# A decode kernel's last sums: result columns taken from every fourth weight column, turned by VectorE in blocks of 32 in place of TensorE

## The chip, the cores and the metric

The kernel runs on one core of a Trainium2 chip. The metric is the device time in microseconds (us) of one execution. Lower is better. A profile of one execution (busy times, waits, transfers) stands beside the timed runs.

## What is computed

One token passes through attention over a cache and through a small MLP, and a gate mixes the two results. Cut to what matters, with x of 512 values, 32 heads of 128, 4096 cached keys and F = 1376:

```python
g = sigmoid((x * gate_w).sum(-1))
q = (x @ wq) as 32 heads of 128
p = softmax(q . k_cache * 128 ** -0.5)        # per head, over 4096 keys
a = (p . v_cache) as 4096 values @ wo         # wo: 4096 x 512
h = relu(x @ w1 + b1) ** 2                    # w1: 512 x 1376
b = h @ w2 + b2                               # w2: 1376 x 512
out = g * a + (1 - g) * b                     # 512 values, bf16
```

## The kernel before

**Stages.** Nearly all the work is reading the two caches and the weights, 78 MB in bf16. The 32 heads go in eight groups of four ("q" 0 to 7). For each group the keys K and the values V come as one transfer each of 4096 KB into two buffers for K and two for V; the list ORDER gives the sequence K0 K1 V0 K2 K3 V1 and so on up to V7. All of these, the loads of w1, wo and w2, and the write of the result are issued by SyncE (SP) in the order of its program. A load of K or V waits until the buffer's former content has been used, and what stands behind it in SP's program waits with it. wo comes in four quarters of 1024 KB: three go into one slot, each waiting for the products of the quarter before (s_wd), the last into a slot of its own. V7 comes in three pieces. After it SP issues the last quarter of wo and the five pieces of w2 (W2_PARTS: two of 512 KB, the remainder of 96 KB, two of 128 KB) with no wait between them, and then waits for s_f4, the sign that the result is ready to be written.

**TensorE** turns part of the keys (L460), forms their scores (L467), sums the values (pv, L501) and, for each pair of groups, turns the finished heads (turn, L519), spreads them over 128 partitions (spread, L525) and multiplies them with a quarter of wo (out_rows, L534). VectorE forms the scores of the other keys (L685 and L689) and ScalarE evicts the turned keys (L355) and takes the exponentials (L372).

**The last products.** The 512 results live as four columns of 128 partitions in the PSUM tile acc (pQ, columns 256 to 260): column j holds results 128 j to 128 j + 127. Each product is a pair: TensorE loads a block of 128 x 128 weights as the stationary operand and sends one column of activations through it, so the block's 128 columns become 128 partitions of one column of acc. out_rows(a) makes 32 such pairs for a quarter of wo. mlp_out(c) makes four for each row group of w2 in piece c. Both add into acc. At the end out_rows(1) and mlp_out(0) to mlp_out(4) follow each other on TensorE, each mlp_out waiting for its piece of w2.

Behind the last pair, VectorE adds the scaled second bias b2g to acc and writes accs, [128, 4] in bf16 (L756). TensorE turns accs into acc4, four rows of 128 in PSUM (L646), VectorE copies these into fin4 (L758), and SP writes fin4 to the output (L282): row j goes to results 128 j and up.

**The bias.** At the start ScalarE issues the small loads. b2r receives B_b2 as four rows of 128 (L329); it lies in the space of w1_sb, so SP's load of w1 (L271) waits for s_b2. TensorE turns b2r into four columns B2 of PSUM (L608) behind the first query products and ahead of the first keys; VectorE scales B2 by 1 - g into b2g (L673).

**Loads of weights with their columns apart.** Two places take a stationary operand whose columns are not neighbours in memory: the four matmuls that turn x into columns, xrow[:, t:DM:4] on one partition (L594), and the first MLP product, w1_sb[:, t, n:FG * 128:FG] with FG = 10 (L513), with its bias b1r[:, n:FG * 128:FG] (L509).

Of the kernel before, what the change touches and what calls it, by code (L numbers as in the profile page):

```python
# [5 lines left out]
def bass_gated_mix__gqa_block_cached__dense_activation_squared_relu__decode_kernel(  # L6
# [16 lines left out]
    bf16 = mybir.dt.bfloat16  # L23
# [6 lines left out]
    DM = 512  # L30
# [49 lines left out]
    with ctx:  # L80
        def sb(name, shape, dt):
            return ctx.enter_context(nc.sbuf_tensor(name, shape, dt))

        def pb(name, shape, dt):
            return ctx.enter_context(nc.psum_tensor(name, shape, dt))

        def sem(name):
            return ctx.enter_context(nc.semaphore(name))
# [5 lines left out]
        wo_sb = W[:, 0:2 * TB * DM].rearrange("p (g t n) -> p g t n", g=2, t=TB)  # L94
# [4 lines left out]
        w1_sb = sb("w1_sb", [128, 4, F], bf16)  # L99
# [7 lines left out]
        xrow = w1_sb[0:1, 0, 0:DM]  # L107
        grow = w1_sb[0:1, 1, 0:DM]
        b1r = sb("b1r", [1, F], bf16)
        b2r = w1_sb[0:4, 2, 0:128]  # L110
        oT = sb("oT", [GH, 128], bf16)
        o2 = sb("o2", [128, TB], bf16)
        fin4 = sb("fin4", [4, 128], bf16)
        zeros = sb("zeros", [128, 128], bf16)
        xb = sb("xb", [128, 4, 128], bf16)
        ident = sb("ident", [128, 128], bf16)
# [19 lines left out]
        hs = sb("hs", [128, FG + 1], bf16)  # L136
        b2g = sb("b2g", [128, 4], fp32)
        accs = sb("accs", [128, 4], bf16)
# [4 lines left out]
        pO = pb("pO", [128, 512], fp32)  # L143
# [6 lines left out]
        OT = KP[2][0:GH, 0:128]  # L150
        O2 = KP[3][:, 0:2 * TB].bitcast(fp32)
        Z = pO[:, 76:77]
        B2 = pO[:, 78:80].bitcast(bf16)
        acc4 = pO[0:4, 128:192].bitcast(bf16)
        QR = [pQ[:, :]] + [p[:, :].bitcast(fp32) for p in KP[0:3]] + [pQ[:, :]] * (NQ - QF)
        H = KP[0][:, 0:2 * (FG + 1)].bitcast(fp32)
        acc = pQ[:, 256:260]
# [3 lines left out]
        s_b = sem("s_b")  # L161
# [21 lines left out]
        s_b2 = sem("s_b2")  # L183
# [27 lines left out]
        s_oc = sem("s_oc")  # L211
        s_acc = sem("s_acc")
        s_as = sem("s_as")
        s_fin = sem("s_fin")
        s_f4 = sem("s_f4")
        s_out = sem("s_out")

# [11 lines left out]
        @block.sync  # L229
        def _(eng):  # L230
            def load_kv(n):
                kind, q = ORDER[n]
                if q >= 2:
                    done(kind, q - 2)
                if kind == "K":
                    eng.dma_start(KV[:, K_SLOT[q], :], k_q[q, :, :]).then_inc(s_k[q], 16)
                else:
                    at = 0
                    for m, sv in zip(V_PARTS[q], s_v[q]):
                        a, b = at * PB * 128, (at + m) * PB * 128  # L240
                        eng.dma_start(KV[:, V_SLOT[q], a:b], v_q[q, :, a:b]).then_inc(sv, 16)  # L241
                        at += m

            def done(kind, q):
                if kind == "K":
                    eng.wait_ge(s_sd, NP * (q + 1))
                    eng.wait_ge(s_t, GQ * (q + 1))
                else:
                    eng.wait_ge(s_pv, q + 1)

            def load_wo(g):
                if g == 0:
                    eng.wait_ge(s_qps, NQ)
                elif g < NG - 1:
                    eng.wait_ge(s_wd, g)
                a = 0 if g < NG - 1 else 1
                eng.dma_start(wo_sb[:, a, :, :], wo_v[g, :, :, :]).then_inc(s_wo[a], 16)  # L257

            def load_w2(n):
                a, b = W2_PARTS[n]  # L260
                if a < FG:
                    eng.dma_start(w2a[:, a:b, :], w2_v[:, a:b, :]).then_inc(s_w2[n], 16)  # L262
                else:
                    eng.dma_start(w2b[:, :], B_w2[FG * 128:F, :]).then_inc(s_w2[n], 16)  # L264

            for n in range(len(ORDER)):
                load_kv(n)
                if n == 2:
                    eng.wait_ge(s_z, 1)
                    eng.wait_ge(s_b2, 1)  # L270
                    eng.dma_start(w1_sb[:, :, :], w1_v[:, :, :]).then_inc(s_w1, 16)  # L271
                if n in WO_AT:
                    load_wo(WO_AT[n])
            load_wo(NG - 1)
            eng.wait_ge(s_sd, NP * NQ)
            load_w2(0)
            load_w2(1)
            load_w2(2)
            load_w2(3)
            load_w2(4)  # L280
            eng.wait_ge(s_f4, 1)
            eng.dma_start(out[0, 0, :].rearrange("(j p) -> j p", p=128), fin4[:, :]).then_inc(s_out, 16)  # L282


        @block.gpsimd
# [35 lines left out]
        def _(eng):  # L321
# [4 lines left out]
            eng.dma_start(xrow, A_x[0, :, :]).then_inc(s_x, 16)  # L326
            eng.dma_start(grow, gate_w.rearrange("(a n) -> a n", a=1)).then_inc(s_gw, 16)
            eng.dma_start(b1r[:, :], B_b1.rearrange("(a n) -> a n", a=1)).then_inc(s_b, 16)
            eng.dma_start(b2r, B_b2.rearrange("(j p) -> j p", p=128)).then_inc(s_b, 16)  # L329
            eng.wait_ge(s_xc, 1)  # L330
            eng.activation(xcolf[:, :], XC, ACT.Copy).then_inc(s_xf, 1)  # L331
            eng.wait_ge(s_xf, 1)
# [75 lines left out]
        def _(eng):  # L408
# [45 lines left out]
            def take(sm, n=1):  # L454
                eng.wait_ge(sm, n).then_inc(sm, -n)  # L455
# [73 lines left out]
            def out_rows(a):  # L529
                take(s_oc)  # L530
                take(s_wo[a], 16)
                for t in range(TB):
                    for j in range(4):
                        mm = eng.matmul(acc[:, j:j + 1], wo_sb[:, a, t, j * 128:(j + 1) * 128], o2[:, t:t + 1],  # L534
                                        start=False, stop=False, skip_group_check=True)
                mm.then_inc(s_wd, 1)

            def mlp_out(c, last=False):
                eng.wait_ge(s_w2[c], 16)
                a, b = W2_PARTS[c]  # L540
                for n in range(a, b):
                    M = 128 if n < FG else FR
                    w = w2a[:, n, :] if n < FG else w2b[:, :]
                    for j in range(4):
                        mm = eng.matmul(acc[:, j:j + 1], w[:, j * 128:(j + 1) * 128], hs[0:M, n:n + 1],  # L545
                                        start=False, stop=last, skip_group_check=True)
                if last:
                    mm.then_inc(s_acc, 1)
# [33 lines left out]

            at("rows")
            out_rows(0)
            branch("IS_GE", LAST, "next", "rows2")
            at("rows2")
# [6 lines left out]
            for t in range(4):  # L593
                mm = eng.matmul(XC[:, t:t + 1], xrow[:, t:DM:4], ident[0:1, 0:1], start=True, stop=True)  # L594
# [10 lines left out]
            eng.wait_ge(s_qc, QF)  # L605
            eng.wait_ge(s_b, 32)
            eng.wait_ge(s_ez, 1)
            eng.transpose(B2, b2r, ident[0:4, 0:4]).then_inc(s_b2, 1)  # L608

            part("k0")  # L610
            keys(0, extra[0])
# [24 lines left out]
            turn()  # L636
            spread()
            out_rows(1)
            eng.wait_ge(s_hs, 2)
            mlp_out(0)  # L640
            mlp_out(1)
            mlp_out(2)
            mlp_out(3)
            mlp_out(4, last=True)
            eng.wait_ge(s_as, 1)
            eng.transpose(acc4, accs[:, :], ident[:, :]).then_inc(s_fin, 1)  # L646


        @block.vector
        def _(eng):  # L650
# [20 lines left out]
            def bias():  # L671
                eng.wait_ge(s_b2, 1)
                eng.tensor_scalar(b2g[:, :], B2, omg[:, 0:1], None, ALU.mult).then_inc(s_bg, 1)  # L673

# [79 lines left out]
            eng.wait_ge(s_acc, 1)  # L754
            eng.wait_ge(s_bg, 1)
            eng.tensor_tensor(accs[:, :], acc[:, 0:4], b2g[:, :], ALU.add).then_inc(s_as, 1)  # L756
            eng.wait_ge(s_fin, 1)
            eng.tensor_copy(fin4[:, :], acc4).then_inc(s_f4, 1)  # L758

        body.close()  # L760
        nc.sync.wait_ge(s_out, 16)
# [28 lines left out]
```

## Time and profile before

| what | value |
|---|---|
| time, median of 3 runs | 190.74 us (190.69 to 190.84) |
| the profiled execution: its time | 190.55 us |
| its span, first to last instruction | 189.2 us |
| TensorE matmuls, busy | 137.1 us (72%) |
| TensorE weight loads, busy | 119.8 us (63%) |
| VectorE, busy | 123.0 us (65%) |
| ScalarE, busy | 116.0 us (61%) |
| read from HBM | 78.32 MB, 414 GB/s over the span |
| packets of SP's and ScalarE's loads (queue q1), share of 16 DMA engines | 97.1% |
| mean granted TensorE clock | 0.735 |
| in the last stage (184 to 187.5 us) | 0.50 |

Busy time counts an engine's instructions; PE is TensorE's matmuls and PEld its weight loads, which overlap. DVE is VectorE, ACT ScalarE, SPq SyncE's issuing of transfers. "out<-in" names the written and the read tile, "128*128" the size of the stationary operand, and in brackets stands how long the engine had been idle before and what ended that. The granted clock is a share of TensorE's full clock.

### The profile page before, as it was taken

The page shows a single profiled execution, that of the slowest core. Times are in us where ns is not written, and L with a number is a line of the kernel's source. Part 1 is how long each engine was busy: PE and PEld are TensorE (multiplying, and loading weights), DVE is VectorE, ACT ScalarE, POOL GpSimd, SP SyncE. Part 2 cuts the span into 40 slices and gives each one's busy share as a digit, 9 for nine tenths or more (in the row PEclk, how much of TensorE's full clock was granted, in tenths as well). Part 3 has the DMA queues.
Part 4 walks back from the last instruction along what each step waited for, and adds up shares of the span by engine and source line. Part 5 has one row for each costly group of instructions (what it writes and reads, how often), then busy time and mean ns, then how long its engine had stood idle before and what let it go on. Part 6 is the DMA issues. An engine that isn't in the chain of part 4 may idle for free. (4 is left out here: it accounts for less than half of the span.)

```text
span 189.2 us, 6234 instructions
## 1 busy us (share of the span) xinstructions
PE 137.1 (72%) x2688; PEld 119.8 (63%) x2688; DVE 123.0 (65%) x123; ACT 116.0 (61%) x243; POOL 6.0 (3%) x13
## 2 busy tenths in 40 slices
PE   0009297668849979969968797829868496889865
PEld 0003165537739779758958696829767495879864
DVE  0110099979969999996998299919990499701010
ACT  3004559948989986984987099708973298560000
POOL 4000000000700000000000000000000000000000
PEclk9999969958975975995795559655985579555555
DMA  6999999989989999999999999999999999999992
GB/s 225 437 444 443 443 443 426 443 361 483 440 360 436 443 443 440 417 436 430 443 424 409 423 443 443 436 436 436 414 445 409 416 443 443 438 388 416 421 388 78
DMA packets 4177, 78.47 MB, mean 415 GB/s; under 512 B 483, under 2 KB 837, under 8 KB 1094
## 3 DMA queue, kind: packets, MB, share of 16 engines
q1 hardware_dynamic: 4152, 78.32, 97.1%
q8 instruction: 7, 0.11, 0.2%
q14 instruction: 4, 0.03, 0.0%
q10 hardware_dynamic: 14, 0.01, 0.0%
HBM read 78.32 MB, written 0.00 MB: 414 GB/s over the span
## 5 line engine op out<-in xcount | busy, mean ns | idle before, releaser
L355 ACT ACTIVATE kT<-KP 128x1024 bf16<-128x1024 bf16 x80 | 75.3, 1041 | 26.1 <-PE KP L460 25.9
L685 DVE TENSOR_TENSOR w2a<-KV,qb 128x1536 f32<-128x1536 bf16 x32 | 56.3, 1760 | 19.4 <-DMA KV<-in_A_k_cache_dram 19.0
L460 PE MATMUL KP<-ident,KV 128*128 128x128 bf16 x640 | 59.6, 256 | 10.5 <-PEq L455 10.5
L460 PEld LDWEIGHTS KP<-ident,KV 128*128 128x128 bf16 x640 | 48.4, 116 | 14.1 <-issue 13.1
L689 DVE TENSOR_REDUCE S<-w2a 128x12 f32<-128x1536 f32 x32 | 56.1, 1753 | 1.1
L467 PE MATMUL pS<-qc,kT 128*128 128x4 bf16 x640 | 28.1, 166 | 13.0 <-PEq L455 11.0
L467 PEld LDWEIGHTS pS<-qc,kT 128*128 128x128 bf16 x640 | 24.6, 99 | 18.9 <-issue 17.6
L501 PEld LDWEIGHTS pO<-E,KV 128*128 128x128 bf16 x1024 | 29.3, 105 | 0.0
L501 PE MATMUL pO<-E,KV 128*128 128x4 bf16 x1024 | 28.4, 166 | 0.0
L372 ACT ACTIVATE E<-S,nM 32x128 bf16<-32x128 f32 x32 | 18.5, 578 | 0.9
L445 PE MATMUL pQ<-W,xb 128*128 128x512 bf16 x20 | 7.8, 532 | 7.2 <-DMA W<-in_A_wq_dram 6.1
L338 ACT ACTIVATE qb<-pQ 32x128 bf16<-32x128 f32 x20 | 5.4, 268 | 9.7 <-PE pQ L445 9.3
L361 ACT ACTIVATE S<-pS 32x80 f32<-32x80 f32 x32 | 7.3, 228 | 4.8 <-PE pS L467 4.2
L445 PEld LDWEIGHTS pQ<-W,xb 128*128 128x128 bf16 x20 | 2.2, 126 | 9.6 <-DMA W<-in_A_wq_dram 6.2
L372 ACT ACTIVATION_READ_ACCUMULATOR E<-S,nM 32x1 f32 x32 | 8.1, 252 | 0.0
L664 DVE TENSOR_SCALAR e<-ez 128x1 f32<-128x1 f32 x1 | 0.2, 153 | 10.8 <-ACT ez L387 10.8
L708 DVE RECIPROCAL rden<-pO 128x4 f32<-128x4 f32 x8 | 1.4, 174 | 8.2 <-PE pO L501 8.2
L594 PE MATMUL pO<-ident,w_sb 1*128 1x1 bf16 x4 | 0.3, 165 | 7.8 <-DMA w_sb<-in_A_x_dram 7.8
L497 PE MATMUL pO<-RS,onesf 128*128 128x4 f32 x16 | 4.3, 339 | 1.8 <-PEq L455 1.8
L655 DVE TENSOR_SCALAR xb<-zeros,xcolf 128x128 bf16<-128x128 bf16 x4 | 0.7, 248 | 7.5 <-ACT xcolf L331 7.5
L488 PE MATMUL pM<-identf,mp 128*1 128x128 f32 x8 | 3.0, 372 | 3.4 <-PEq L455 3.1
L497 PEld LDWEIGHTS pO<-RS,onesf 128*128 128x128 f32 x16 | 3.8, 298 | 2.1 <-issue 2.0
(75 smaller groups left out, 72.2 us busy)
## 6 DMA issues: line engine op xcount, KB each, us to landing
KV<-in_A_k_cache_dram SPq DMA_DIRECT2D x8, 4096.0 KB, 22.0
KV<-in_A_v_cache_dram SPq DMA_DIRECT2D x7, 4096.0 KB, 29.5
W<-in_A_wq_dram SPq DMA_DIRECT2D x1, 4096.0 KB, 13.4
W<-in_A_wo_dram SPq DMA_DIRECT2D x4, 1024.0 KB, 16.5
KV<-in_A_v_cache_dram SPq DMA_DIRECT2D x1, 2048.0 KB, 11.0
KV<-in_A_v_cache_dram SPq DMA_DIRECT2D x2, 1024.0 KB, 14.1
w_sb<-in_B_w_dram SPq DMA_DIRECT2D x1, 1376.0 KB, 24.4
w2a<-in_B_w_dram SPq DMA_DIRECT2D x2, 512.0 KB, 18.5
```

Of the source, the lines that this page charges most:

```text
L338: eng.activation(qb[rows(r), c, :], QR[c][rows(r), r * 128:(r + 1) * 128], ACT.Copy)\
L355: eng.activation(kT[:, n % NT, :], KP[n % NKP][:, :], ACT.Copy).then_inc(s_ev, 1)
L361: eng.activation(S[rows(r), q % NS, 0:YQ], S2[rows(r), :, r], ACT.Copy).then_inc(s_cp, 1)
L372: eng.activation(E[rows(r), q % 2, :, r], S[rows(r), q % NS, :], ACT.Exp, bias=nM[rows(r), q:q + 1], scale=SCALE, accum_out=RS[rows(r), q ...
L445: mm = eng.matmul(QR[c], xb[:, t, :], wq_sb[:, t, c * 512:(c + 1) * 512], start=(t == 0), stop=(t == 3))
L460: mm = eng.transpose(KP[(GQ * a + g) % NKP][:, y * 128:(y + 1) * 128], key(a, b), ident[:, :])
L467: mm = eng.matmul(pS[:, R * c:R * c + R], kT[:, (GQ * a + g) % NT, y * 128:(y + 1) * 128], qc2[:, a, :], start=True, stop=True)
L488: eng.transpose(MT, mp[:, a:a + 1], identf[:, :]).then_inc(s_mt, 1)
L497: eng.matmul(DEN[a], onesf[:, :], RS[:, a, :], start=True, stop=True)
L501: mm = eng.matmul(O[a], KV[:, V_SLOT[a], b * 128:(b + 1) * 128], E[:, a, COLUMN[b], :], start=(b == 0), stop=(b == NB - 1))
L685: eng.tensor_tensor(prod, KV[:, K_SLOT[q], x:x + XB * 128].rearrange("p (b d) -> p b d", d=128), qb[:, q, :].unsqueeze(1).to_broadcast([12 ...
L689: eng.tensor_reduce(S[:, q % NS, c:c + XB], prod, AX.X, ALU.add).then_inc(s_sd, 1)
```

## The change

Result column j of acc now takes the weight columns j, j + 4, j + 8 and so on of wo and w2, in place of the columns 128 j to 128 j + 127. Partition m, column j thus holds result 4 m + j, and the 32 partitions of a block hold 128 results in order. VectorE turns accs in blocks of 32 x 32: its source is each of the four columns repeated 32 times, so block j has 32 equal columns; its destination is written with a step of four values. Row 32 k of fin then holds results 128 k to 128 k + 127 (the other rows repeat them), and SP writes the rows 0, 32, 64 and 96. TensorE's last turn, VectorE's copy and the semaphore s_fin are gone; VectorE waits for its own L756 in their place. The bias has to have the same order: b2r is loaded as one row of 512, and four matmuls against a 1 x 1 one bring every fourth value into a column of B2, now in fp32.

```diff
-        b2r = w1_sb[0:4, 2, 0:128]
+        b2r = w1_sb[0:1, 2, 0:DM]
...
-        fin4 = sb("fin4", [4, 128], bf16)
+        fin = sb("fin", [128, 128], bf16)
...
-        B2 = pO[:, 78:80].bitcast(bf16)
-        acc4 = pO[0:4, 128:192].bitcast(bf16)
+        B2 = pO[:, 78:82]
...
-            eng.dma_start(out[0, 0, :].rearrange("(j p) -> j p", p=128), fin4[:, :]).then_inc(s_out, 16)
+            eng.dma_start(out[0, 0, :].rearrange("(k n) -> k n", k=4), fin[0:128:32, :]).then_inc(s_out, 16)
...
-            eng.dma_start(b2r, B_b2.rearrange("(j p) -> j p", p=128)).then_inc(s_b, 16)
+            eng.dma_start(b2r, B_b2.rearrange("(a n) -> a n", a=1)).then_inc(s_b, 16)
...
-                        mm = eng.matmul(acc[:, j:j + 1], wo_sb[:, a, t, j * 128:(j + 1) * 128], o2[:, t:t + 1],
+                        mm = eng.matmul(acc[:, j:j + 1], wo_sb[:, a, t, j:DM:4], o2[:, t:t + 1],
                                         start=False, stop=False, skip_group_check=True)
...
-                        mm = eng.matmul(acc[:, j:j + 1], w[:, j * 128:(j + 1) * 128], hs[0:M, n:n + 1],
+                        mm = eng.matmul(acc[:, j:j + 1], w[:, j:DM:4], hs[0:M, n:n + 1],
                                         start=False, stop=last, skip_group_check=True)
...
-            eng.transpose(B2, b2r, ident[0:4, 0:4]).then_inc(s_b2, 1)
+            for j in range(4):
+                mm = eng.matmul(B2[:, j:j + 1], b2r[:, j:DM:4], ident[0:1, 0:1], start=True, stop=True)
+            mm.then_inc(s_b2, 1)
...
-            eng.wait_ge(s_as, 1)
-            eng.transpose(acc4, accs[:, :], ident[:, :]).then_inc(s_fin, 1)
...
-            eng.wait_ge(s_fin, 1)
-            eng.tensor_copy(fin4[:, :], acc4).then_inc(s_f4, 1)
+            eng.wait_ge(s_as, 1)
+            eng.transpose(fin[:, :].rearrange("p (i j) -> p j i", j=4),
+                          accs[:, :].rearrange("p (j a) -> p j a", a=1).broadcast_to([128, 4, 32]))\
+               .then_inc(s_f4, 1)
```

More of the change, by code (lines that the diff above doesn't have):

```diff
@@ L213, in bass_gated_mix__gqa_block_cached__dense_activation_squared_relu__decode_kernel @@
         s_as = sem("s_as")
-        s_fin = sem("s_fin")
         s_f4 = sem("s_f4")
```

## The prediction, made before the changed kernel was run

> **What bounds the kernel now.** I read the page's span and engine shares first, then the chain of work that ended last in order of time, then the timeline of the last 14 us, and last the rows of weight loads whose columns lie apart. The profiled execution took 190.55 us: a span of 189.2 us and 1.35 us around it. The median of the runs shown is 190.74, so what the sum gains or loses on the profiled execution I carry over to that median, 0.19 us above it.
>
> ```profile
> span 189.2 us, 6234 instructions
> ...
> DMA 10%; PE 2%; SPq 2%; issue 0%; DVE 0%
> ```
>
> The chain has almost no engine work in it. In order of time (start, us, what) it ends so:
>
> ```profile
> 168.56 18.33 DMA w2a<-in_B_w_dram
> 186.90 0.05 issue
> 186.94 0.28 PE pQ L545 x4
> 187.22 0.02 issue
> 187.25 0.17 DVE accs L756
> 187.42 0.04 issue
> 187.46 0.28 PE pO L646
> 187.75 0.02 issue
> 187.77 0.21 DVE fin L758
> ```
>
> The transfers bound the kernel until the last piece of w2 lands at 186.90. Behind it only a short tail is serial: four matmuls, the bias add, TensorE's turn, its copy, the write. A change counts if it alters this tail, or if it makes TensorE come later than the landing. How far TensorE is ahead is in the timeline:
>
> ```profile
> 176.49 0.94 PEld L534 LDWEIGHTS pQ<-o,W 128*128 128x128 bf16 x32
> ...
> 184.32 0.94 PEld L534 LDWEIGHTS pQ<-o,W 128*128 128x128 bf16 x32 [0.56 <-issue]
> ...
> 185.18 0.50 PEld L545 LDWEIGHTS pQ<-hs,w2a 128*128 128x128 bf16 x16
> ...
> 186.06 0.50 PEld L545 LDWEIGHTS pQ<-hs,w2a 128*128 128x128 bf16 x16 [0.38 <-DMA w2a<-in_B_w_dram]
> ...
> 188.01 0.33 SPq L282 DMA_DIRECT2D out_dram<-fin  x1
> ```
>
> One load lasts 0.104 us (the median at L534), but they overlap: 32 take 0.94 us, so they stand (0.94 - 0.104) / 31 = 0.027 us apart. Call this spacing s. All the work at L534 and L545 is such pairs of one load and a one-column matmul.
>
> **The tail that is replaced.** From the end of L756 (187.42) to the issue of the write (188.01) lie 0.59 us: 0.04 to start, 0.28 for the turn at L646, 0.02, 0.21 for the copy at L758, 0.03. Afterwards there is 0.04 (one VectorE instruction waiting for the one before: L708 ends at 182.21 and L716 starts at 182.25), VectorE's turn T, and 0.03. No turn on VectorE is in the trace, so T has bounds. Below: the copy that goes, 128 elements on 4 partitions in 0.21. Nearest in size: L655, 128x128 bf16 to bf16 in 0.248. Above: a row that writes bf16 values 8 bytes apart, as the turn does:
>
> ```profile
> L372 ACT ACTIVATE E<-S,nM 32x128 bf16<-32x128 f32 x32 | 18.5, 578 | 0.9
> ...
> L655 DVE TENSOR_SCALAR xb<-zeros,xcolf 128x128 bf16<-128x128 bf16 x4 | 0.7, 248 | 7.5 <-ACT xcolf L331 7.5
> ```
>
> That is ScalarE and an exponential, so 0.58 is far off. I take T = 0.28: L655 plus the filling of one block of 32, at L685's pace of 1760 / 1536 = 1.15 ns an element about 0.04. The tail then takes 0.04 + 0.28 + 0.03 = 0.35 and saves 0.24 us; with T at its bounds it saves 0.31 or loses 0.06. [...]
>
> **The weights' columns, every fourth.** Result column j now loads columns j, j+4, ... of wo and w2, so neighbours lie 8 bytes apart. The count stays: 4 x 32 pairs at L534 and 44 at L545. What such a load costs is bounded by two rows, both of this timeline:
>
> ```profile
> 7.78 0.20 PEld L594 LDWEIGHTS pO<-ident,w_sb 1*128 1x128 bf16 x4 [7.78 <-issue]
> ...
> 168.00 0.31 PEld L513 LDWEIGHTS KP<-xcol,w_sb 128*128 128x128 bf16 x4
> ```
>
> L594 loads xrow[:, t:DM:4], the same step of 8 bytes, but on one partition: loads of 0.108 (median), spacing (0.20 - 0.11) / 3 = 0.030 us. L513 loads w1 with a step of FG = 10, 20 bytes, on 128 partitions: spacing (0.31 - 0.136) / 3 = 0.058 by the loads, and by its matmuls (four in 0.39, one 0.197) 0.064; I say 0.062. The lower bound is s = 0.027, nothing. I take 0.031, since L594 has the step itself and only the partitions differ; the bias loads at L509, one partition at the step of 20 bytes, last 0.132 against 0.157 at L513, so partitions matter less than the step (L594 against L534: 0.108 to 0.104).
>
> [...]
>
> The granted clock differs: 1.00 around L594 (7.0 to 8.5), 0.50 in the tail. If a step of 8 bytes cost a number of TensorE's cycles, 0.030 would become 0.06 there. Against that, TensorE was not yet at full pace at L594: its matmuls of 512 columns at L445 stand 0.43 apart from 14.61 to 16.74, under a granted 1.00, and later 0.21.
>
> What s = 0.031 moves: the first two groups at L534 (105.22 and 144.36) end 0.13 later, and SP's wo loads at 106.25 and 145.38 and the V loads behind them go out as much later. The work in flight hides that: K7 and V5 (4096 KB each) were issued at 122.55 and 123.65, TensorE begins on K7 only at 149.2, and V5 is still behind it, so the queue isn't empty at 145.5. The third group (176.49) pushes pv(7), the turn and the spread by 32 x 0.004 = 0.13, so the fourth starts at 184.45. Before the last four matmuls stand 32 + 16 + 16 + 4 + 4 = 72 pairs. Without waits for DMA these would be through at 184.32 + 72 x 0.027 = 186.26 before, against a start of the last four at 186.94: 0.68 us of cover. Now: 184.45 + 72 x 0.031 = 186.68, cover 0.26. From the landing at 186.06 on: 24 x 0.031 gives 186.80, cover 0.14. So TensorE still waits for the last landing, and on the path lie only three gaps of the last four: 3 x 0.004 = 0.01 us.
>
> **The bias.** One turn of 4x4 (L608, 21.93) becomes four matmuls of L594's kind: 3 x 0.031 = 0.09 us more on TensorE. It hides in the 1.96 us that TensorE then waits for K0 (L460 starts at 24.08); without that, 0.09. SP's load of w1 (L271) waits for it; it goes out at 22.3 in place of 22.22, behind K0, K1 and V0 still in flight. The w1 load has K2 behind it, which waits for buffers until 38.28 anyway. The load of b2, one row of 1 KB in place of four of 256 bytes, is issued at 3.38 and used at 21.9: hidden. VectorE's scaling at L673 (0.211) reads fp32 in place of bf16, near L722's 0.169: at 43.2, off the chain.
>
> **The write.** Four rows of 256 bytes as before, from partitions 32 apart. No row shows a difference; I take 0 and bounds of 0.1 both ways, well inside the 1.2 us from its issue to the end of the span.
>
> **Sum.** -0.24 + 0.01 = -0.23 us: 190.32 on the profiled execution, 190.51 against the median.
>
> **Rivals.**
>
> *TensorE becomes the bound of the tail (slower).* If loads 8 bytes apart on 128 partitions cost as those at L513, the place is L534 at 184.32 and all behind it. The delay is 104 (s - 27) ns (32 pairs of the third group, 72 before the last four) less 676 of cover, plus 3 (s - 27). Against the 240 saved, break-even is 916 / 107 = 8.6 above 27: from s = 36 ns on the kernel is slower, from 39 by over 0.2%. At 62: 3.64 - 0.68 + 0.11 - 0.24 = +2.83 us, 193.6. For it: L513 is the only load with its columns apart on all partitions, and L594's clock is in doubt. Against it: L594 has the step. Middle of the case, s = 45: +1.01, 191.7.
>
> *VectorE's turn costs what it replaces (no change).* T at 0.5 to 0.6, by the row of L372: saved 0.02 or lost 0.08, 190.7 to 190.8. For it: a write 8 bytes apart and a source read 32 times over, neither shown on VectorE. Against it: L338, ScalarE's dense copy of 128, takes 0.268, and much of L372's 0.58 can be the exponential.
>
> *The last landing moves.* The rate falls from 311 GB/s (184.0 to 184.5) to 33 (186.5 to 187.0), as some of the 16 engines finish before others; shifted issues at 106 and 145 may alter who is last, by some 0.4 us either way: 190.1 or 190.9. For it: the slope. Against it: the three runs lie within 0.15 us.
>
> **How the numbers follow.** Forecast 0.50, TensorE the bound 0.21, turn as dear 0.14, landing moved 0.15. A measurement of this kernel tells about 0.2% from no change, 0.38 us; the forecast is 0.12%. Faster by more needs a gain of 0.38: 0.15 of the forecast's chance (T near 0.21 with a little from the write) and 0.08 of the moved landing, 0.23. Slower: 0.20 of TensorE's case and 0.07 of the landing, 0.27. Within: 0.35 + 0.14 + 0.01 = 0.50. The forecast's own range is 190.3 to 190.7. The whole range reaches down to 190.2 and up to 191.8 (s = 46), which leaves out the far half of TensorE's case and the best of the landings.
>
> **What would show it.** Right: L534's loads at 0.99 to 1.1 us for 32, an idle gap before the last four at L545 that DMA ends, the turn at 0.25 to 0.35, the write issued about 0.24 after the old distance from the last landing. Wrong: groups at L534 of 1.3 us or more with no idle TensorE from 184.3 to the end; a turn of over 0.5; or a last landing that has moved by more than 0.3.

## The result, and the profile after

The changed kernel takes 191.32 us (median of nine runs, 191.13 to 191.75) against 190.84 for the kernel before beside it: a ratio of 1.0027 with a 95% interval of 1.0017 to 1.0036. It is slower by some 0.5 us, where the forecast was 0.23 faster. The profiled execution took 191.40, against 190.55 of the kernel before: 0.85 us apart, more than the medians, so the trace holds something besides the change.

The chain of work that ended last, of the changed kernel (start, us, what). L532, L543, L754 and L280 are L534, L545, L756 and L282 of before; VectorE's turn is L758.

```profile
184.67 1.20 PE pQ L532 x32
185.87 0.53 PE pQ L543 x16
...
186.41 1.17 PE pQ L543 x28
...
187.60 0.17 DVE accs L754
...
187.80 0.46 DVE fin L758
```

The wait for w2, 18.33 us long in the chain of before, isn't in this one: TensorE's 76 pairs are, and the add behind them starts 0.35 us later (L754 at 187.60, L756 at 187.25). But the chain and the timeline pass over short pauses. The last four loads by themselves, of the changed kernel and then of the kernel before:

```profile
187.27 0.21 PEld L543 LDWEIGHTS pQ<-hs,w2a 128*128 128x128 bf16 x4
186.94 0.18 PEld L545 LDWEIGHTS pQ<-hs,w2a 128*128 128x128 bf16 x4
```

In the changed kernel they start 0.10 us after the load ahead of them, where loads otherwise stand 0.033 apart; in the kernel before it was 0.24, with the others 0.027 apart. In the traces the last piece of w2 lands at 187.23 and, before, at 186.90, each time 0.04 us ahead of these four. So TensorE still waits for w2, 0.07 us in place of 0.21, and 0.33 of the 0.35 us are a later landing. Then come the lines of the timeline:

```profile
181.30 0.93 PEld L499 LDWEIGHTS pO<-E,KV 128*128 128x128 bf16 x32 [0.37 <-issue]
...
184.64 1.14 PEld L532 LDWEIGHTS pQ<-o,W 128*128 128x128 bf16 x32 [0.56 <-issue]
187.60 0.16 DVE L754 TENSOR_TENSOR accs<-pQ,b2g 128x4 bf16<-128x4 f32 x1 [3.23 <-PE pQ L543]
187.80 0.46 DVE L758 STREAM_TRANSPOSE fin<-accs 128x128 bf16<-128x128 bf16 x1
188.29 0.64 SPq L280 DMA_DIRECT2D out_dram<-fin  x1
```

Three things are to be seen. The first line is the values' product: TensorE stood idle for 0.37 us before its last 32 blocks, which in the trace of before it did not; the last piece of V7 landed at 181.14, before at 180.82. The last block of pairs at L532 takes 1.14 in place of 0.94. And the write, the last line, is issued in 0.64 us in place of 0.33. The span ends at 190.0, 1.71 us behind the start of that issue; before it was 189.2 - 188.01 = 1.19. So the difference of the spans is made of 0.35 (TensorE's end), -0.07 (L754's start to the write's issue: 0.69 in place of 0.76) and +0.52 (the write): 0.80 us. The spans are given to 0.1 us here; the traces have 189.97 and 189.21, by which the write is +0.48 and the sum 0.76. Without the landing's 0.33 that is 0.43, near the 0.48 us between the medians. Which of these belongs to the change, and which to one execution?

### The profile page after: what moved, and what is told of

Read it like the earlier page. It is cut to its first block, busy times and chain, and to the rows that moved or that the text cites. A ratio compares the mean times of both kernels' runs of the same rounds, so it can differ in the third digit from the quotient of the medians.

```text
span 190.0 us, 6235 instructions
## 1 busy us (share of the span) xinstructions
PE 138.0 (73%) x2687; PEld 121.0 (64%) x2690; DVE 123.2 (65%) x123; ACT 116.0 (61%) x243; POOL 6.0 (3%) x13
## 5 line engine op out<-in xcount | busy, mean ns | idle before, releaser
L443 PE MATMUL pQ<-W,xb 128*128 128x512 bf16 x17 | 6.7, 528 | 7.8 <-DMA W<-in_A_wq_dram 6.4
L532 PE MATMUL pQ<-o,W 128*128 128x1 bf16 x128 | 4.8, 172 | 0.5 <-PEq L453 0.5
```

Of the source, the lines that this page charges most:

```text
L443: mm = eng.matmul(QR[c], xb[:, t, :], wq_sb[:, t, c * 512:(c + 1) * 512], start=(t == 0), stop=(t == 3))
L532: mm = eng.matmul(acc[:, j:j + 1], wo_sb[:, a, t, j:DM:4], o2[:, t:t + 1], start=False, stop=False, skip_group_check=True)
```

## The experiments

Theory W: the write of rows that lie 32 partitions apart is what the change pays for. Theory C: the dearer weight loads made TensorE late, as the chain above by itself would have it. Theory I: the longer issue is no matter of the rows, but of an instruction fetch, since 164 GB/s moved for a tenth of a microsecond at 187.9 with all loads done.

### One part at a time

**Rows 0 to 3 written, in the changed kernel.**

```diff
-eng.dma_start(out[0, 0, :].rearrange("(k n) -> k n", k=4), fin[0:128:32, :])
+eng.dma_start(out[0, 0, :].rearrange("(k n) -> k n", k=4), fin[0:4, :])
```

> The changed kernel, but the write takes rows 0 to 3 of fin in place of rows 0, 32, 64 and 96 (all rows of a block are equal, so the output then holds results 0 to 127 four times). Theory W, the write of rows 32 partitions apart is what the change paid for (issue 0.64 us in place of 0.33, data moving 1.26 us after the issue in place of 0.74): the issue is 0.33 again, issue to end of span 1.2 in place of 1.7, and the time 0.5 us under the changed kernel, so -0.02 us against the kernel before (190.8). Theory C, TensorE's dearer weight loads made it late: the time stays 0.4 to 0.5 us over the kernel before. Theory I, the longer issue came from an instruction fetch at 187.9 us and not from the rows: the issue is still 0.6.

Measured: 190.77 us, ratio to the kernel before 0.9995 (0.9986 to 1.0004). The loss is gone with the step over partitions. The timeline of this kernel, its last two rows:

```profile
188.20 0.46 DVE L758 STREAM_TRANSPOSE fin<-accs 128x128 bf16<-128x128 bf16 x1
188.69 0.33 SPq L280 DMA_DIRECT2D out_dram<-fin  x1
```

The issue is back at 0.33, and to the end of the span (189.9) it is 1.21. This execution was a late one (191.23 us, 0.46 over the median): w2 landed at 187.62, and the turn starts at 188.20. The median is at that of the kernel before.

**The weight columns alone, in the kernel before.**

```diff
-wo_sb[:, a, t, j * 128:(j + 1) * 128]
+wo_sb[:, a, t, j:DM:4]
...
-w[:, j * 128:(j + 1) * 128]
+w[:, j:DM:4]
```

> The kernel before with the weight columns alone changed to every fourth (the results come out in another order, as the tail is the old one). Theory W: loads 0.033 us apart are mostly covered by the wait for the last piece of w2; at most +0.1 us against the kernel before. Theory C: +0.3 to +0.4 us, as the profile of the changed kernel had TensorE's last pair 0.36 later, and no wait for DMA behind 184.6.

Measured: 190.78 us, ratio 0.9996 (0.9985 to 1.0006). Theory C expected 0.3 to 0.4 us more and falls. Its timeline:

```profile
184.45 1.12 PEld L534 LDWEIGHTS pQ<-o,W 128*128 128x128 bf16 x32 [0.56 <-issue]
...
186.99 0.21 PEld L545 LDWEIGHTS pQ<-hs,w2a 128*128 128x128 bf16 x4
187.32 0.16 DVE L756 TENSOR_TENSOR accs<-pQ,b2g 128x4 bf16<-128x4 f32 x1 [3.13 <-PE pQ L545]
```

TensorE waits for w2 here as well: the last piece lands at 186.94, 0.04 us ahead of the last four pairs. The add starts at 187.32, 0.07 later than in the trace of before, and 0.05 of that is the landing.

**The tail alone, in the kernel before.**

```diff
-eng.transpose(acc4, accs[:, :], ident[:, :])     # TensorE
-eng.tensor_copy(fin4[:, :], acc4)                # VectorE
+eng.transpose(fin[:, :].rearrange("p (i j) -> p j i", j=4),
+              accs[:, :].rearrange("p (j a) -> p j a", a=1).broadcast_to([128, 4, 32]))
...
-eng.dma_start(out[0, 0, :].rearrange("(j p) -> j p", p=128), fin4[:, :])
+eng.dma_start(out[0, 0, :].rearrange("(k n) -> k n", k=4), fin[0:128:32, :])
```

> The kernel before with the tail alone changed: VectorE's turn and the write of rows 32 apart, dense weight columns (the results come out in another order). Theory W: the tail from the last matmul to the write's issue saves 0.07 us and the write loses 0.5, together +0.4 us. Theory C: -0.07 us or so, as the weights are dense.

Measured: 191.32 us, ratio 1.0023 (1.0011 to 1.0034). That is the whole loss, with dense weights. The turn takes 0.46 and the issue 0.64 here as well; the issue starts at 188.18 and the span ends at 189.8, 1.62 later.

**The write alone, in the kernel before.**

```diff
-eng.dma_start(out[0, 0, :].rearrange("(j p) -> j p", p=128), fin4[:, :])
+eng.dma_start(out[0, 0, :].rearrange("(j p) -> j p", p=128), ident[0:128:32, :])
```

> The kernel before, unchanged up to the sign that the result is ready; the write then takes rows 0, 32, 64 and 96 of the identity matrix in place of the four rows of the result (so the output isn't the result). Theory W: issue 0.64 us in place of 0.33, +0.5 us against the kernel before. Theory C and theory I: no change.

Measured: 191.46 us, ratio 1.0036 (1.0024 to 1.0049). The write alone loses all of it and perhaps a little more. The timeline of this kernel shows a tail as in the kernel before, up to its last row:

```profile
187.76 0.21 DVE L758 COPY fin<-pO 4x128 bf16<-4x128 bf16 x1 [0.36 <-PE pO L646]
188.00 0.64 SPq L282 DMA_DIRECT2D out_dram<-ident  x1
```

Theory W holds in all four; theories C and I, which expected no change of this one, fall. Theory I has more against it: the DMA view shows one packet of 16 KB of instructions near the end of the changed kernel's trace, at 187.99, and such a packet also stands at 187.87 in the trace with rows 0 to 3 and at 187.75 with the columns alone, where the issue took 0.33.

### What makes the write dear: the distance, or the step?

**Rows 0, 2, 4 and 6, in the kernel before** (`ident[0:8:2, :]` as the source).

> The kernel before; the write takes rows 0, 2, 4 and 6 of the identity matrix in place of the result's four rows (the output isn't the result). If it is any step over partitions that costs: issue 0.64 us and 0.5 to 0.6 us over the kernel before, as with rows 32 apart. If it is the distance of 32, or that the rows lie in four blocks of 32 partitions: issue 0.33 and no change.

Measured: 191.51 us, ratio 1.0028 (1.0008 to 1.0049).

```profile
188.41 0.73 SPq L282 DMA_DIRECT2D out_dram<-ident  x1
```

The issue takes 0.73, and the span ends 1.79 behind its start. Four rows within seven partitions are as dear as four rows 32 apart: it is the step, not the distance. The step doesn't make more packets: the DMA view counts eight for the write with and without it, four of 256 bytes and four of 4. What grows is the time from the start of the issue to the first data, 1.2 to 1.3 us in place of 0.75. What is done in it, no run shows.

**Four writes of one row, two on SP and two on ScalarE, in the changed kernel.**

```diff
+# SP: k = 0, 1; ScalarE, after its last exponential: k = 2, 3
+eng.dma_start(out[0, 0:1, 128 * k:128 * k + 128], fin[32 * k:32 * k + 1, :])
```

> The changed kernel with its write cut into four of one row, two issued by SP and two by ScalarE, which is idle by then; no transfer steps over partitions. If the step over partitions is what costs: issues of 0.3 each, two behind each other, data moving at 0.33 + 0.75 = 1.1 us after the first, and a time 0.1 to 0.2 us under the changed kernel. If it is the rows' place in SBUF: no gain, or a loss of 0.3 from the second issue.

Measured: 191.18 us, ratio 1.0014 (1.0003 to 1.0025) where the changed kernel had 1.0027; the two intervals overlap. The issues:

```profile
188.25 0.31 SPq L280 DMA_DIRECT2D out_dram<-fin  x1
188.25 0.23 ACTq L405 DMA_DIRECT2D out_dram<-fin  x1
188.51 0.26 ACTq L406 DMA_DIRECT2D out_dram<-fin  x1
188.60 0.29 SPq L281 DMA_DIRECT2D out_dram<-fin  x1
```

Without the step no issue takes over 0.31, though the rows are at the same places. The second issue takes back most: 1.65 us from the first issue to the end of the span (189.9).

**The sums written as they are, with no turn, in the changed kernel.**

```diff
-eng.transpose(...)
-eng.dma_start(out[0, 0, :].rearrange("(k n) -> k n", k=4), fin[0:128:32, :])
+eng.dma_start(out[0, 0, :].rearrange("(p j) -> p j", j=4), accs[:, :])
```

> The changed kernel without VectorE's turn: partition m of accs holds results 4 m to 4 m + 3, so SP writes accs itself, 128 rows of 8 bytes. Saved: the turn, 0.46 us and 0.04 before it. Theory W1, the write is dear because its rows' partitions step by more than one, not because it has rows: rows on neighbouring partitions are issued in 0.33, and the time is 0.5 + 0.5 under the changed kernel, about 190.3, that is 0.5 under the kernel before. Theory W2, each row of a small write costs of its own: 128 rows of 8 bytes take 1 us or more longer than 4 of 256, and the time is at or above the changed kernel's 191.3.

Measured: 192.06 us, ratio 1.0056 (1.0038 to 1.0074). Both theories were right in a part. The rows are on neighbouring partitions and the issue is short; what is long is the wait behind it. The timeline's row of the issue, and from the view of SP's waits its wait for this write (us in all, times, longest):

```profile
187.77 0.35 SPq L280 DMA_DIRECT2D out_dram<-accs  x1
```

```profile
SPq L759 <- DMA out_dram<-accs: 2.3, 1, 2.3
```

The kernel before waits 0.5 there. By the transfer rates in steps of 0.05 us, all data of this write moves between 188.60 and 188.85, and the span ends at 190.8, 1.95 us later; in the kernel before the data moves by 188.85 too, and the span ends 0.35 later.

### What makes the turn long

**Eight instructions in VectorE's idle time at 11 to 14 us, in the changed kernel.**

```diff
+f4, ac = fin[:, :].rearrange("p (i j) -> p j i", j=4), accs[:, :]
+f1 = fin[:, :].rearrange("p (j i) -> p j i", j=4)
+ab = ac.rearrange("p (j a) -> p j a", a=1).broadcast_to([128, 4, 32])
+z4 = zeros[:, :].rearrange("p (j i) -> p j i", j=4)
+# turns: (f4, ab) (f1, ab) (f4, z4) (f1, z4) (fin[:, 0:32], zeros[:, 0:32])
+# copies: (f4, z4) (f1, z4) (f1, ab)
```

> The changed kernel with eight extra instructions in VectorE's idle time at 11 to 21 us, on the tiles fin, accs and zeros, each waiting for the one before: five turns (source repeated and destination with a step of four, as in the change; source repeated and destination dense; source dense and destination with the step; both dense; one block of 32 both dense), then three copies of 128x128 (destination with the step; both dense; source repeated). Theory D, the step in the destination makes the turn long: 0.46 with it, 0.28 without, whatever the source, and the copy with the step is longer too. Theory S, the repeated source does it: 0.46 with it, 0.28 with a dense source. Theory B, a turn is long by itself: all four of 128 columns at 0.46, one block at 0.25 or so.

The one run took 191.33 us, as the changed kernel does. The timeline of these, each row by itself:

```profile
10.95 0.46 DVE L738 STREAM_TRANSPOSE fin<-accs 128x128 bf16<-128x128 bf16 x1
11.44 0.31 DVE L738 STREAM_TRANSPOSE fin<-accs 128x128 bf16<-128x128 bf16 x1
...
11.79 0.46 DVE L738 STREAM_TRANSPOSE fin<-zeros 128x128 bf16<-128x128 bf16 x1
12.29 0.31 DVE L738 STREAM_TRANSPOSE fin<-zeros 128x128 bf16<-128x128 bf16 x1
12.63 0.21 DVE L738 STREAM_TRANSPOSE fin<-zeros 128x32 bf16<-128x32 bf16 x1
12.88 0.31 DVE L740 COPY fin<-zeros 128x128 bf16<-128x128 bf16 x1
13.22 0.20 DVE L742 COPY fin<-zeros 128x128 bf16<-128x128 bf16 x1
```

Theory D: the step in the destination makes it 0.46, a dense one 0.31, whatever the source. A copy pays for the step too, 0.31 in place of 0.20. The repeated source costs a turn nothing (and a copy 0.03: it took 0.23).

### Versions without the step over partitions

After the turn the 32 rows of a block are equal, so each may be the one that is written. Rows 31 and 32 are neighbours and belong to two blocks, and so are 95 and 96.

**Rows at the edges of blocks, in the changed kernel.**

```diff
+# SP: h = 0; ScalarE, after its last exponential: h = 1
+eng.dma_start(out[0, 0, 256 * h:256 * h + 256].rearrange("(k n) -> k n", k=2),
+              fin[64 * h + 31:64 * h + 33, :])
```

> The changed kernel with another choice of rows to write. After the turn all 32 rows of a block are equal, so rows 31 and 32 hold the first two quarters of the result and rows 95 and 96 the last two: SP writes rows 31 and 32, ScalarE rows 95 and 96, each two neighbouring partitions. If the step over partitions is the whole cost of the write: issues of 0.33 or less side by side, issue to end of span 1.2 us, and 0.4 to 0.6 us under the changed kernel, which is at the kernel before or up to 0.1 under it (190.75 to 190.85). If a write over two blocks of 32 partitions, or a second queue, costs too: 191.0 or more.

Measured: 190.92 us, ratio 0.9995 (0.9982 to 1.0009). The loss is gone, and no gain can be told; the time is a little over the 190.75 to 190.85 that was expected. The issues take 0.32 and 0.26, and the end of the span (189.4) lies 1.34 behind them, where one write of four neighbouring rows had 1.19 to 1.22: the second queue isn't free.

**The same with a dense turn** (`fin[:, :].rearrange("p (j i) -> p j i", j=4)` as the destination).

> As the one with rows at the edges of blocks, but the turn's destination is dense, without the step of four (the results come out in another order within each quarter). The turn takes 0.31 us in place of 0.46, as measured in the idle time, and it stands alone on the tail: the time is 0.15 us under the one with the step, 0.15 to 0.25 under the kernel before. This is what the change would have brought with a turn at the length assumed (0.28) and a write without the step; if TensorE's dearer loads cost time in most runs, it is less than 0.1 under the kernel before.

Measured: 190.64 us, ratio 0.9989 (0.9980 to 0.9998): 0.2 us under the kernel before, as expected. The trace accounts for half of it: from the add to the issue it saves 0.22 (0.54 in place of 0.76), and the write on two queues gives back 0.11 (1.30 in place of 1.19). The interval holds both.

**Dense weights, a dense turn, and runs of 32 results, in the kernel before.** Row 32 k of the turned sums then holds results 32 k to 32 k + 31 of each of the four columns, and the write puts these runs in place.

```diff
+# SP: h = 0; ScalarE, after its last exponential: h = 1
+eng.dma_start(out[0, 0, :].rearrange("(j k i) -> k j i", j=4, k=4)[2 * h:2 * h + 2],
+              fin[64 * h + 31:64 * h + 33, :].rearrange("k (j i) -> k j i", j=4))
```

> The kernel before with another tail: dense weight columns and the old bias; VectorE turns the sums in blocks of 32 into a dense destination (0.31 us), so row 32 k holds four runs of 32 results, 128 apart; SP writes rows 31 and 32, ScalarE rows 95 and 96, 16 runs of 64 bytes in all. Theory P, only the step over partitions made the write dear: issue to end of span 1.2 to 1.4 us, and the tail's saving of 0.2 us shows, 190.5 to 190.75. Theory Q, short pieces are dear too (128 rows of 8 bytes had needed 2.3 us of waiting behind the issue): more than 1.5 us from issue to end, and 191.0 or more.

Measured: 190.70 us, ratio 0.9990 (0.9978 to 1.0002). From the timeline:

```profile
187.48 0.16 DVE L756 TENSOR_TENSOR accs<-pQ,b2g 128x4 bf16<-128x4 f32 x1 [3.30 <-PE pQ L547]
187.67 0.31 DVE L758 STREAM_TRANSPOSE fin<-accs 128x128 bf16<-128x128 bf16 x1
188.01 0.33 SPq L282 DMA_DIRECT2D out_dram<-fin  x1
188.02 0.27 ACTq L406 DMA_DIRECT2D out_dram<-fin  x1
```

From the add to the issue it is 0.53 in place of 0.76, and from there to the end of the span (189.4) 1.39 in place of 1.19: about 0.2 gained and 0.2 given back in this execution. The median is 0.1 us under the kernel before, but the interval still holds 1. These 16 runs of 64 bytes on two queues aren't as dear as the 128 rows of 8 on one (190.8 - 187.77 = 3.03 from the issue to the end of the span); whether by their size or their number isn't shown. This version has the result in order with the old weights and the old bias, and no loss against the kernel before can be told.

## Why the prediction failed

**The step that failed is "The write": "I take 0 and bounds of 0.1 both ways".** It measured +0.5 us in the trace (1.71 in place of 1.19 from issue to end), 0.31 of it in the issue (0.64 in place of 0.33) and the rest between the issue and the first data. The prediction counted rows and bytes, which stayed, and didn't ask what else the transfer's form had changed. No row of the trace had a step over partitions, and a case without a row wanted bounds as wide as the tail. The measured time lies inside the range of 190.2 to 191.8, but by luck: for a cause that was no rival. Counted from the landing, the terms of the sum came out so: the tail -0.07 in place of -0.24, the weights +0.02 in place of +0.01 (0.37 us from the landing to the add, where it was 0.35), the write +0.48 in place of 0. That is +0.43 in place of -0.23, and the medians differ by 0.48.

**VectorE's turn** was mis-sized: 0.46 for a forecast of 0.28. The bound above, 0.58 by ScalarE's row with the same step, was the better neighbour: the extra turns show that the step in the destination is what it pays for. The tail up to the write saved 0.07 in place of 0.24. With a dense destination it took 0.31, near the 0.28. The 0.04 in that forecast for the filling of a block was an estimate from L685's pace; no run shows such a filling.

**The weight loads** were nearly right: spaced (1.14 - 0.118) / 31 = 0.033 us (0.118 is the median load at L532) where 0.031 was said and 0.027 was the dense price; the row of one partition at L594 was the right neighbour, and L513's 0.062 was not. The doubt about the clock is answered too: at the granted 0.50 of the tail the spacing is 0.033, not 0.06. On 128 partitions the step of 8 bytes costs 6 ns on 27 here, where the 20 bytes at L513 cost 35; what sets either, no run shows.

**TensorE's cover** held, as the prediction said, though it came out small. Counted from the landing of the second piece of w2 on, 0.14 us were to be left ahead of the last four pairs; 0.07 were left in the changed kernel's trace and 0.03 with the columns alone. In seven of the eight traces with the new columns the last four pairs start 0.04 us behind the last landing, as in all five with dense ones. Only in the trace of the sums written as they are was TensorE itself late, by 0.03. The prediction's own formula says how near it was: 104 x (33 - 27) = 624 of the 676 ns of cover are used up. By the medians the new columns cost nothing that can be told (0.9985 to 1.0006 with the columns alone).

**The last landing**, a rival of its own, was 0.33 us later in the changed kernel's profiled execution, which is over the 0.3 named as a sign. It isn't shown to be the change's: the landing wanders from 186.89 to 187.30 in the five traces with dense columns and from 186.94 to 187.62 in the eight with the new ones. In this execution all was late by then: V6 landed at 171.27 in place of 170.94, and the 0.37 us of idle TensorE in the values' product end 0.15 behind the landing of V7's last piece. The slope that was given for this rival was misread in part: w2's data ends by 186.50, and the 33 GB/s from 186.5 to 187.0 are one packet of instructions.

**The bias** was hidden as said: L607's four matmuls take 0.26 us at 22.58, and TensorE then waits 1.21 us for K0.

## What to carry to other kernels

Look at the form of the last transfer, not only at its rows and bytes: here the write's 0.48 us in the trace stood in full in the time (0.48 between the medians), and the 0.07 that the tail without TensorE had saved were handed back there. Where a step over partitions is wanted, look for neighbours that hold the same data, as the equal rows of a block do here; the repeated source that makes them cost the turn nothing (0.31 us with it and without). Before a wait is called gone, look at the starts of single instructions: a merged row can hide a short one (0.07 us here). A price for which no row exists wants a bound from the nearest odd form, or a place among the rivals; "as before" holds only for what is the same in every dimension.

## What the runs showed of the hardware that was not expected

- A write of four rows of 256 bytes with a step over partitions (2 or 32) is issued in 0.64 to 0.73 us, from neighbouring partitions in 0.33; from issue to the end of the span it takes 1.62 to 1.79 us against 1.19 to 1.22, with the same number of packets.
- A write of 128 rows of 8 bytes is issued in 0.35 us, its data has moved 1.1 us after the start of the issue, but the span ends 1.95 us after that, where four rows of 256 bytes need 0.35.
- Two writes side by side on two queues end 1.30 to 1.39 us behind their issue, 0.1 to 0.2 later than one write of the same four rows, though each is issued in 0.33 or less.
- On VectorE a destination step of four bf16 values costs 0.15 us in a turn of 128x128 (0.46 in place of 0.31) and 0.11 in a copy (0.31 in place of 0.20).
